# Decay tables of a recurrent-attention-plus-MLP kernel fetched as eight rows and spread by TensorE, and one rounding operation moved ahead of a read-out

## Chip, cores, metric

One core of one Trainium2 chip. The metric is device time in microseconds of one execution. All executions counted here are of the fast state (the one execution of the ladder has no state on record), and "the kernel before" is always the one run beside the others on the same chip. Three chips occur: one for the first comparison, one for the first four experiments, one for the other eight.

## The reference

A recurrent attention with a decay per head, whose output is the input of an MLP with leaky ReLU:

```python
gamma = 1.0 - 2.0 ** (-5.0 - np.arange(H, dtype=np.float32))
for t in range(S):                      # B, H, S, D = 4, 8, 768, 64
    state = gamma[None, :, None, None] * state + np.einsum('bhd,bhe->bhde', k[:, :, t], v[:, :, t])
    y[:, :, t] = scale * np.einsum('bhd,bhde->bhe', q[:, :, t], state)
# x = y as (3072, 512)
h = x @ w_in                            # 512 x 2048, given in float64
g = np.maximum(0.01 * h, h)
out = (g @ w_out).astype(np.float32)
```

## The kernel before

The sequence is worked in chunks of 128 tokens (C). The decays become three constant tables in one tile `dec` of 128 x 524 values: `gq` (512 columns, one per query position for each of four pairs of heads), `gk` (8 columns) and `gc` (4 columns). Start-up is a race: TensorE has nothing to multiply until queries and keys land, and the first projection step ("d", `direct`) needs both attention outputs and weights. The weights come as float64 words and are rounded to float32 by ScalarE (`powers`) and VectorE (`mantissas`), piece by piece. Fillers (`keep_busy`, on zeros) are there to bring TensorE's clock up.

```python
    load_qk(0, 0)
    nc.sync.dma_start(out=dec[:, rates:], in_=decay[:, rates:])     # gk, gc: 128 rows of 48 bytes
    load_v(0, 0)
    load_qk(0, 1)
    nc.sync.dma_start(out=dec[:, :rates], in_=decay[:, :rates])     # gq: 128 rows of 2 KB
    load_v(0, 1)
    load_piece(0)
    load_qk(0, 2)
    load_v(0, 2)
    load_piece(1)
    # ... cut
    keep_busy(7)
    score(0, 0)             # 16 matmuls on 64x64 quarters of the array
    masked(0, 0)            # VectorE, PSUM -> SBUF
    decay_v(0, 0, nc.vector)   # values times gk
    keep_busy(6)
    score(0, 1)
    values(0, 0)
    masked(0, 1)
    decay_v(0, 1, nc.vector)
    keep_busy(3)
    next_powers()           # ScalarE, weights piece 0
    taken(0, 0, x)          # the read-out: x = PSUM times gq
    values(0, 1)
    taken(0, 1, x)
    next_powers()
    next_mantissas()        # VectorE, three operations on piece 0
    score(0, 2)
    keep_busy(3)
    steps = direct(0, 0, x, parts[0][1], 0)
    next(steps)             # first d step
    next_mantissas()
    # ... cut: the second d step needs weights piece 1, and so on
```

## Time and profile before

| | before |
|---|---|
| median (3 runs) | 668.73 us (668.72 to 668.85) |
| time of the profiled execution | 669.81 us, span 667.9 us |
| TensorE busy | 660.5 us, 99% of the span |
| TensorE busy from 18.29 us to the end | 646.05 of 649.60 us |
| first d step, second d step | 16.00 us, 18.29 us |

Here is the start of TensorE's own timeline (start, length, engine, line, operation, what it writes and reads, array rows and columns used, shapes, count, idle time before):

```profile
1.40 3.17 PE L610 MATMUL idle<-t 128*128 128x512 bf16 x7 [1.40 <-DVE t L605]
4.49 1.99 PE L165 MATMUL ap<-qk 64*64 64x128 f32 x32
6.41 1.67 PE L610 MATMUL idle<-t 128*128 128x512 bf16 x6
```

Seven fillers took 3.17 us, the next six 1.67 us. The page's clock row prints full rate where it has no record yet.

### The profile page before, as it was taken

The page shows a single profiled execution, that of the slowest core. Times are in us where ns is not written, and L with a number is a line of the kernel's source. Part 1 is how long each engine was busy: PE and PEld are TensorE (multiplying, and loading weights), DVE is VectorE, ACT ScalarE, POOL GpSimd, SP SyncE. Part 2 cuts the span into 40 slices and gives each one's busy share as a digit, 9 for nine tenths or more (in the row PEclk, how much of TensorE's full clock was granted, in tenths as well). Part 3 has the DMA queues.
Part 4 walks back from the last instruction along what each step waited for, and adds up shares of the span by engine and source line. Part 5 has one row for each costly group of instructions (what it writes and reads, how often), then busy time and mean ns, then how long its engine had stood idle before and what let it go on. Part 6 is the DMA issues. An engine that isn't in the chain of part 4 may idle for free.

```text
span 667.9 us, 10403 instructions
## 1 busy us (share of the span) xinstructions
PE 660.5 (99%) x4507; PEld 573.1 (86%) x4507; DVE 371.9 (56%) x570; ACT 175.5 (26%) x321; POOL 19.6 (3%) x21
## 2 busy tenths in 40 slices
PE   7999999999999999999999999999999999999998
PEld 4888888888888888888888888888888888888886
DVE  4789869889889685314542613653531444341342
ACT  2864456255261002111201310210211220221210
POOL 0000000000000111000000100100100000000000
PEclk9999999999999999999999999999999999999999
DMA  8931322322421553003002200301300000000001
GB/s 320 405 113 32 121 69 64 98 92 65 157 64 65 189 190 127 1 0 104 25 16 82 93 1 1 127 1 64 127 1 0 2 0 33 31 1 1 0 1 63
DMA packets 16029, 49.17 MB, mean 74 GB/s; under 512 B 1904, under 2 KB 2160, under 8 KB 15984
## 3 DMA queue, kind: packets, MB, share of 16 engines
q1 hardware_dynamic: 15984, 48.51, 20.9%
q8 instruction: 35, 0.57, 0.3%
q14 instruction: 10, 0.08, 0.0%
HBM read 42.21 MB, written 6.29 MB: 73 GB/s over the span
## 4 chain that ended last, share of the span: by engine, by line
PE 97%; DMA 1%; SPq 1%; DVE 1%; ACT 0%; issue 0%; DVEq 0%
PE B_o L398 12%; PE A_o L398 12%; PE C_o L398 12%; PE C_h L398 12%; PE B_h L398 12%; PE A_h L398 12%; PE D_o L398 6%; PE D_h L398 6%; PE yp L193 3%; PE ap L165 3%; PE d L420 2%; PE yp L184 2%; DMA raw<-in_weights_dram 1%; PE yp L208 1%; PE sums L208 0%; SPq L134 0%
## 5 line engine op out<-in xcount | busy, mean ns | idle before, releaser
L398 PE MATMUL A_h<-x,w 128*128 128x256 f32 x368 | 86.9, 379 | 0.0
L398 PEld LDWEIGHTS A_h<-x,w 128*128 128x128 f32 x368 | 69.9, 190 | 9.5
L398 PE MATMUL A_o<-g,w 128*128 128x256 f32 x288 | 68.0, 379 | 0.0
L433 ACT ACTIVATE g<-g 128x512 f32<-128x512 f32 x69 | 42.0, 630 | 89.3 <-DVE g L347 89.3
L398 PEld LDWEIGHTS A_o<-g,w 128*128 128x128 f32 x288 | 54.7, 190 | 7.4
L438 ACT COPY m<-A_h 128x512 f32<-128x512 f32 x23 | 13.4, 583 | 141.2 <-PE A_h L398 101.6
L347 DVE TENSOR_TENSOR m<-m,B_h 128x512 f32<-128x512 f32 x23 | 15.7, 685 | 57.7 <-PE B_h L398 57.7
L347 DVE TENSOR_TENSOR m<-m,B_o 128x512 f32<-128x512 f32 x16 | 10.9, 684 | 63.9 <-PE B_o L398 63.9
L398 PE MATMUL C_h<-t,w 128*128 128x256 f32 x184 | 44.1, 382 | 0.0
L398 PE MATMUL B_h<-x,w 128*128 128x256 f32 x184 | 44.1, 382 | 0.0
L238 DVE TENSOR_TENSOR x<-yp,dec 128x512 f32<-128x512 f32 x24 | 16.4, 688 | 48.6 <-PE yp L208 34.2
L398 PE MATMUL B_h<-t,w 128*128 128x256 f32 x184 | 43.5, 379 | 0.0
L398 PE MATMUL C_h<-x,w 128*128 128x256 f32 x184 | 43.5, 379 | 0.0
L398 PE MATMUL D_h<-t,w 128*128 128x256 f32 x184 | 43.5, 379 | 0.0
L398 PEld LDWEIGHTS C_h<-t,w 128*128 128x128 f32 x184 | 34.5, 190 | 5.5 <-issue 0.9
L398 PEld LDWEIGHTS D_h<-t,w 128*128 128x128 f32 x184 | 35.0, 190 | 4.8
L398 PEld LDWEIGHTS C_h<-x,w 128*128 128x128 f32 x184 | 35.0, 190 | 4.8
L398 PEld LDWEIGHTS B_h<-t,w 128*128 128x128 f32 x184 | 35.0, 190 | 4.8
L398 PEld LDWEIGHTS B_h<-x,w 128*128 128x128 f32 x184 | 34.5, 190 | 5.1 <-issue 0.3
L350 DVE TENSOR_TENSOR gd<-g,gd 128x512 f32<-128x512 f32 x48 | 34.7, 722 | 1.6
L170 DVE TENSOR_TENSOR am<-ap,mask 128x1024 f32<-128x1024 f32 x24 | 28.5, 1219 | 12.0 <-PE ap L165 12.0
L398 PE MATMUL D_o<-gd,w 128*128 128x256 f32 x144 | 34.0, 379 | 0.0
(110 smaller groups left out, 1018.8 us busy)
## 6 DMA issues: line engine op xcount, KB each, us to landing
raw<-in_weights_dram SPq DMA_DIRECT2D x31, 512.0 KB, 4.0
qk<-in_qk_dram SPq DMA_DIRECT2D x19, 512.0 KB, 3.6
kv<-in_kv_dram SPq DMA_DIRECT2D x17, 512.0 KB, 4.6
out_dram<-o SPq DMA_DIRECT2D x23, 256.0 KB, 2.1
in<-in_qk_dram SPq DMA_DIRECT2D x3, 512.0 KB, 7.2
in<-in_kv_dram SPq DMA_DIRECT2D x3, 512.0 KB, 7.8
kv<-in_kv_dram SPq DMA_DIRECT2D x4, 256.0 KB, 7.5
o_in<-in_qk_dram SPq DMA_DIRECT2D x2, 512.0 KB, 9.0
```

The lines of the kernel that those rows point to most:

```text
L165: nc.tensor.matmul(ps[ts(u, 64), j, a, :], lhsT=x[ts(j, 64), 1, a, ts(u, 64)], rhs=x[ts(j, 64), 0, a, :])
L170: nc.vector.tensor_tensor(out=am.rearrange("p j a t -> p (j a) t"), in0=scores[c, b].rearrange("p j a t -> p (j a) t"), in1=mask.unsqueeze ...
L184: nc.tensor.matmul(ps[ts(i, 64), j, m, :], lhsT=st[b][ts(j, 64), a, :], rhs=x[ts(j, 64), 0, a, :], start=(m == 0), stop=False, skip_group_ ...
L193: nc.tensor.matmul(ps[ts(i, 64), j, m, :], lhsT=y[:, 1, 2 * a + j, :], rhs=am[:, j, a, :], start=(c == 0 and m == 0), stop=True, skip_grou ...
L208: nc.tensor.matmul(sp[ts(j, 64), a, :], lhsT=y[:, 0, 2 * a + j, :], rhs=y[:, 1, 2 * a + j, :], start=start, stop=True, skip_group_check=True)
L238: nc.vector.tensor_tensor(out=blocks, in0=ps[:, :, 0 : HP // 2, :], in1=gq, op=ALU.mult)
L347: nc.vector.tensor_tensor(out=out, in0=a, in1=b, op=ALU.add)
L350: nc.vector.tensor_tensor(out=out, in0=a, in1=b, op=ALU.subtract)
L398: nc.tensor.matmul(half, lhsT=block(w, sa)[:, k, ts(i, 128)], rhs=rhs[:, k, :], start=(first and (i == 0 or split) and n == 0 and k == 0), ...
L420: nc.tensor.matmul(banks[r][:, i, :], lhsT=block(2 * u, r + 2 * kh)[:, k, ts(i, 128)], rhs=x[:, 2 * kh + th, k, :], start=(step == 0 and i ...
L433: nc.scalar.activation(g[:, i], g[:, i], AF.Prelu, alpha=0.01)
L438: nc.scalar.copy(out=got["m1"], in_=ps)
```

## The change

The intent: take 262 KB of tables out of the transfers that stand ahead of the first weights. The host now gives eight rows (25 KB) that ScalarE's queue fetches into an unused part of `t`; TensorE multiplies them with rows of ones and zeros and so spreads them over 128 partitions; VectorE and ScalarE copy the results into `dec`. Four fillers go in exchange. Besides, the first of the three rounding operations of weights piece 0 is put ahead of the read-out that waits for TensorE.

```diff
-    load_qk(0, 0)
-    nc.sync.dma_start(out=dec[:, rates:], in_=decay[:, rates:])
-    load_v(0, 0)
-    load_qk(0, 1)
-    nc.sync.dma_start(out=dec[:, :rates], in_=decay[:, :rates])
-    load_v(0, 1)
+    nc.scalar.dma_start(out=rows, in_=decay)
+    load_qk(0, 0)
+    load_v(0, 0)
+    load_qk(0, 1)
+    load_v(0, 1)
 ... cut
-    keep_busy(7)
+    keep_busy(6)
+    nc.tensor.matmul(tables[:, 0, 0:H], lhsT=by_head, rhs=ones, ...)
+    nc.tensor.matmul(tables[:, 0, H : H + HP], lhsT=place, rhs=g_c, ...)
+    nc.vector.tensor_copy(out=dec[:, n_gq:], in_=tables[:, 0, 0 : H + HP])
     score(0, 0)
     masked(0, 0)
+    nc.tensor.matmul(spread, lhsT=place, rhs=g_q, ...)
+    nc.scalar.copy(out=dec[:, 0:n_gq], in_=spread)
     decay_v(0, 0, nc.vector)
-    keep_busy(6)
+    keep_busy(3)
     score(0, 1)
 ... cut
-    taken(0, 1, x)
+    next_mantissas(lambda: taken(0, 1, x))   # first operation, read-out, the other two
     next_powers()
-    next_mantissas()
```

## The prediction

> **What bounds the kernel now.** First the page of the kernel before: which engine is full, and when.
>
> ```profile
> PE 660.5 (99%) x4507; PEld 573.1 (86%) x4507; DVE 371.9 (56%) x570; ACT 175.5 (26%) x321; POOL 19.6 (3%) x21
> ...
> PE   7999999999999999999999999999999999999998
> ...
> DMA  8931322322421553003002200301300000000001
> ```
>
> TensorE is 99% busy; only the first slice (16.7 us) shows a 7, and only there and in the second are the DMA engines at 8 or 9 tenths. A change that touches start-up alone can win only what TensorE lacks there. To find where it starts to run without holes I read the chain of waits of the first 32 us (start, length, what):
>
> ```profile
> 5.72 9.18 DMA raw<-in_weights_dram
> 14.90 0.02 issue
> 14.93 0.67 ACT w L327
> 15.60 0.02 issue
> 15.62 0.64 ACT z L329
> 16.26 0.02 issue
> 16.28 0.44 DVE w L339
> ...
> 16.74 0.70 DVE w L341
> ...
> 17.54 0.70 DVE w L343
> 18.25 0.04 issue
> 18.29 1.99 PE d L420 x8
> 20.28 1.02 PE yp L193 x16
> ```
>
> The reader sees that the end is set by one transfer, the second weight piece. It lands at 14.90, is rounded (ScalarE, then VectorE, 3.35 us), and releases the second step of the first projection, "d", at 18.29. From there on the chain is TensorE after TensorE, with one 1.3 us VectorE piece near 42 us that follows TensorE's own scores. The table of busy time by stretch agrees: from 18.29 to 667.89 TensorE is busy 646.05 of 649.60 us. So **whatever moves that second d step moves the end by as much, until another wait takes over.**
>
> The timeline of VectorE shows what holds the first d step (16.00), the next candidate:
>
> ```profile
> 12.04 0.69 DVE L238 TENSOR_TENSOR x<-yp,dec 128x512 f32<-128x512 f32 x1
> 13.40 0.69 DVE L238 TENSOR_TENSOR x<-yp,dec 128x512 f32<-128x512 f32 x1 [0.68 <-PE yp L193]
> 14.01 0.42 DVE L339 TENSOR_SCALAR w<-raw 128x512 uint32<-128x512 uint32 x1
> 14.46 0.69 DVE L341 SCALAR_TENSOR_TENSOR w<-raw,w 128x512 f32<-128x512 uint32 x1
> 15.26 0.69 DVE L343 SCALAR_TENSOR_TENSOR w<-w,z 128x512 f32<-128x512 f32 x1
> ```
>
> VectorE idles 0.68 us before the second read-out (L238), with the first rounding (L339, L341, L343) queued behind it. Last, the first DMA issues:
>
> ```profile
> 1.24 0.42 SPq L574 DMA_DIRECT2D dec<-decay_dram  x1
> ...
> 2.65 0.43 SPq L577 DMA_DIRECT2D dec<-decay_dram  x1
> ...
> 3.60 0.43 SPq L288 DMA_DIRECT2D raw<-in_weights_dram  x1
> ```
>
> Both tables of decays stand ahead of the first weights. By the times from issue to landing of the single transfers (issue plus landing time): first queries and keys 4.3, small table 4.5, first values 6.1, second queries and keys 9.1, big table 9.75, second values 10.4, first weights 11.7, second weights 14.9.
>
> **What the Trainium skill says.** "DMA: Bandwidth & Descriptors", "Issuing engines are not separate DMA queues": transfers from different issuing engines run on the same 16 DMA engines, and a second issuer saves only sequencer time. The trace before has one queue, so it can't confirm this; it makes me count the bytes removed, not the second queue, as the gain. The same page, "Queues, rings and completion order": on each DMA engine descriptors are taken in ring order. The trace agrees: landings come in the order of issue, and from 8 us on 512 KB take about 1.3 us (11.7, 13.0 for the next two such transfers). The same page, "Why small descriptors are slow (HBM only)" makes the 128 rows of 48 bytes of the small table suspect; but that table landed 0.17 us after the transfer ahead of it, so I count it as little. "TensorE: Matmul & The Clock Gate", "What's actually happening": the array runs at half rate until it has been busy for about 3.4 us, and falls back after an idle window. The trace agrees for the ramp: the first 32 score matmuls took 1.99 us (from 4.49), the next 32 1.10 us (from 9.13). That is what the filler matmuls are for, so I check that the change opens no long hole.
>
> **The change part by part.**
>
> 1. *Table transfers leave the main queue.* Removed: 6 KB in 48-byte rows and 256 KB in 2 KB rows. In the stretch from 8 to 12 us the DMA engines move 418 GB/s with share 1.04, so 262 KB are worth 0.63 us there; the small table lies in a stretch (4 to 8 us) at share 0.84, and I give it 0.1. Added: eight rows of 780 values, 25 KB, 0.06 us at that rate. Net 0.67 us for everything behind the big table in the queue, which includes both first weight pieces. The stretch from 4 to 8 us moved only 290 GB/s; I [...]allow 0.1 us more: **about 0.75 us earlier**, first weights about 10.95, second about 14.15. The second queries and keys have only the small table ahead of them, so I leave them at 9.1 (perhaps 0.2 earlier).
>
> 2. *SyncE issues two transfers fewer* (0.47 us each with their gaps); ScalarE issues one instead, before its table load of 1.28 us, in a time when it is idle until 11.7. The queue is filled well ahead of the data, so this is worth nothing by itself. The waits to reuse a DMA semaphore also shift: the second weights wait for the rows instead of the small table, the third for the first queries and keys; all those land earlier than needed.
>
> 3. *Spreading.* TensorE gets three single-precision matmuls (128x8, 128x4, 128x512) and loses 4 of 19 fillers (7+6+3+3 become 6+3+3+3). A single-precision 128x256 matmul follows the next after 1.73/8 = 0.216 us, so 512 columns are about 0.43 us; three fillers are 3 x 0.278 = 0.83 us (from 1.67 us for six). By my estimate the rows land near 3 us (first packets about 1 us after issue, as for the first transfer[...]), while six fillers end near 4.1, so the scores still start about 4.5. Scores end about 6.5, spread and fillers about 7.8, then TensorE waits for the second queries and keys until 9.1: a hole of 1.3 us where there was one of 1.06. Short of 3.4 us, so the clock should hold. VectorE gets a copy of 12 columns (idle until 6.62), ScalarE a copy of 128x512, 0.58 us as the 128x512 copies of the page, done before 8.5, while the first read-out that needs it is at 12.04. **All of it off the path, 0 us.**
>
> 4. *First rounding's first operation ahead of the second read-out.* It goes into the 0.68 us hole: it can start when VectorE is free at 12.73 and when ScalarE's second pass (which reads what it overwrites) is done. That pass ended 13.05; with weights 0.75 earlier it ends 12.3. So L339 runs 12.7 to 13.1, the read-out stays at 13.40, L341 starts 14.01 instead of 14.46, L343 ends 15.5 instead of 15.95: **first d step at 15.55 instead of 16.00**. Without part 1, L339 would run 13.1 to 13.5 and push the read-out by 0.1.
>
> *Sum.* The second d step needs the later of two: first d step plus its own length, 15.55 + 1.94 = 17.5; and its weights, 18.29 - 0.75 = 17.54. They meet, so the gain is 0.75 us, and part 4 is what lets part 1 through: with the transfers alone the first d step stays near 16.0, the second at 17.95, and the gain is about 0.35. With part 4 alone the second d step still waits for its data: about 0. After it, third weights and the scaling by ScalarE hang on the same chain and the same queue, and move along. Slack there is small (the third d step had its weights at 22.03 and started at 22.27), but it is relative slack, so it stays.
>
> **The rivals.** *A. The gain is held by the front:* the second queries and keys land later (the rows share engines with them) or the hole lets the clock fall, so that scores and values run at half rate (up to 1 us each). Against: 25 KB are 0.06 us, and a hole of 1.06 us did no harm. That would give 668.3 to 669.3. *B. More than the bytes:* the slow stretch from 4 to 8 us was due to the tables, the second queries and keys come 0.5 us or more earlier, and with them the first d step. For it: 290 GB/s against 418. Against: the small table cost 0.17 us. That would give 667.3. *C. Hidden anyway:* later loads or ScalarE's scaling set the third or fourth d step and swallow the gain, giving 668.5. Against: from 18.29 on TensorE has no hole that ends on a transfer. *D. The rows land late* (5 us or more), holding TensorE's queue in front of the scores; harmless up to about 6 us, since the second scores wait until 9.1 anyway.
>
> **Range and chances.** 668.73 - 0.75 = **667.98 us**. Low end: B, 667.4; high end: gain mostly held by a new wait, 668.6; three runs before spread 0.13 us. Two per cent would be 13.4 us, more than all the idle time TensorE has (7.4 us), and no part can cost that: faster by over 2% 0.005, within 2% 0.99, slower by over 2% 0.005.
>
> **What would show it.** Part 1: second weights land near 14.15, first near 10.95. Part 3: rows landed before 4.1, all matmuls after 6.5 at full rate, ScalarE's copy done before 8.5. Part 4: L339 before the second L238, first d step near 15.55. Sum: second d step near 17.55 and no hole of TensorE after it but the one near 42 us; TensorE's busy time from there unchanged near 646 us. Wrong, if the weights land earlier by the bytes and the second d step does not follow, if a new hole opens after it, or if the second queries and keys move by more than 0.3 us.

## The result

The changed kernel took 670.80 us in the median of six runs, the kernel before 668.73 us (now six runs, 668.50 to 669.44); the ratio is 1.0023 (95% interval 1.0004 to 1.0042). That is "same" at 2%, but outside the predicted range, and on the other side. The six runs are not one cluster: five lie at 670.65 to 671.41 us, one at 667.64 us. From here on, "slow" and "fast" executions mean these two clusters.

The changed kernel's page, the lines that answer to the first ones of the prediction:

```profile
PE 663.4 (99%) x4509; PEld 574.8 (86%) x4509; DVE 374.6 (56%) x571; ACT 175.9 (26%) x322; POOL 19.5 (3%) x21
...
PE   9999999999999999999999999999999999999998
```

TensorE's first slice went from 7 to 9. It looks like a better filled engine; it is an engine that takes longer for the same work, as the chain of waits of the first 18 us tells (start, length, what):

```profile
4.13 0.52 PE tables L635 x2
4.65 0.42 PE tables L637 x2
5.07 1.92 PE ap L165 x32
6.99 2.00 PE spread L642 x2
8.99 1.39 PE idle L624 x3
10.38 1.87 PE ap L165 x32
...
16.77 0.70 DVE w L357
...
17.52 3.85 PE d L434 x16
```

There is no transfer left in this chain. The reader is to see three things. The spread took 2.00 us. Three fillers took 1.39 us (six had taken 1.67 before), and the second scores 1.87 us where they took 1.10: the clock was at half rate until about 12 us. And the two d steps run as one (x16, from 17.52): the second follows the first at once, at about 19.4 us, so it no longer waits for its weights but for TensorE. The trace's first record of full rate begins at 11.97 us, against 6.84 before.

The moved operation did what it was moved for (VectorE's timeline):

```profile
14.62 0.42 DVE L346 TENSOR_SCALAR w<-raw 128x512 uint32<-128x512 uint32 x1
15.38 0.69 DVE L238 TENSOR_TENSOR x<-yp,dec 128x512 f32<-128x512 f32 x1 [0.34 <-PE yp L193]
```

And the transfers came much earlier than predicted: second queries and keys 7.55 us (before 9.09), first weights 9.49 (11.70), second weights 12.75 (14.90).

### The profile page after: what moved, and what is told of

Read it like the earlier page. It is cut to its first block, busy times and chain, and to the rows that moved or that the text cites. A ratio compares the mean times of both kernels' runs of the same rounds, so it can differ in the third digit from the quotient of the medians.

```text
span 669.0 us, 10408 instructions
## 1 busy us (share of the span) xinstructions
PE 663.4 (99%) x4509; PEld 574.8 (86%) x4509; DVE 374.6 (56%) x571; ACT 175.9 (26%) x322; POOL 19.5 (3%) x21
## 4 chain that ended last, share of the span: by engine, by line
PE 99%; DVE 1%; issue 0%; DVEq 0%
PE B_o L412 12%; PE A_o L412 12%; PE C_o L412 12%; PE C_h L412 12%; PE B_h L412 12%; PE A_h L412 12%; PE D_o L412 6%; PE D_h L412 6%; PE ap L165 3%; PE yp L193 3%; PE d L434 2%; PE yp L184 2%; PE yp L208 1%; PE idle L624 1%; DVE am L170 0%; PE sums L208 0%
```

## Experiments

**Theory.** The transfers and the order gain, but the matmuls of eight rows keep the clock at half rate, so TensorE's front becomes the bound. **Rivals.** The new order on VectorE costs the time; the fillers that were taken away cost it; the earlier transfers are luck of one trace.

### The transfers and the order without TensorE's part (rows_alone)

```diff
-    (three matmuls and both copies)
+    nc.vector.memset(dec, 0.125)
-    keep_busy(6) ... keep_busy(3)
+    keep_busy(7) ... keep_busy(6)
```

> The transfers of the change and the moved rounding operation, without TensorE's work: the three spreading matmuls and both copies are left out, the fillers are 7 and 6 again, the tables are filled with a constant by VectorE (wrong result on purpose). Theory (the transfers gain about 2 us, and the front of TensorE's queue loses more than that): second queries and keys near 7.6, second weights near 12.8, clock granted near 7 us, second d step near 16.1 to 16.5, so 666.5 to 667.0 us. Rival (the transfers never gain more than the predicted 0.75 us; the earlier landings are luck of one trace): second weights near 14.1, 668.0 us.

Measured: 667.78 us (667.67 to 668.09), kernel before 669.35 (this chip's spread is wider: 668.17 to 670.15), ratio 0.9979 (0.9967 to 0.9991); the result is wrong on purpose. TensorE's timeline:

```profile
7.46 1.10 PE L165 MATMUL ap<-qk 64*64 64x128 f32 x32 [0.29 <-DMA qk<-in_qk_dram]
...
13.88 1.99 PE L434 MATMUL d<-x,w 128*128 128x256 f32 x8 [0.39 <-DVE w L357]
16.36 1.99 PE L434 MATMUL d<-x,w 128*128 128x256 f32 x8 [0.49 <-DVE w L357]
```

The second scores start when their data land and run at full rate, and the second d step starts at 16.36. So the transfers and the order together gain 1.4 us (0.21% of 669), and what the change lost on top of that is TensorE's part with its two copies. The absolute times expected were 1 us too low, because they were counted from the trace before, which was a late one.

### TensorE's part without the transfers (dummy8, dummy128)

The kernel before with the same matmuls as dummies on zeros; the two kernels differ in the number of rows alone.

```diff
-    keep_busy(7); score(0, 0); masked(0, 0); decay_v(0, 0); keep_busy(6)
+    keep_busy(6); single(8); single(4); score(0, 0); masked(0, 0)
+    single(256); single(256); decay_v(0, 0); keep_busy(3)
+    # single(n): lhsT = zeros[0:k, 0:128], rhs = zeros[0:k, 0:n], k = 8 or 128
```

> The kernel before with TensorE's front of the changed kernel put in as dummies on zeros: after 6 fillers two tiny single-precision matmuls of 8 rows, after the first scores two 8-row matmuls of 256 columns, then 3 fillers; transfers as before. Theory (these matmuls keep the clock at half rate): three fillers after the dummies take 1.3 us, second scores take 1.9 us and end near 12.2, second d step near 20, so about 670.5 us. Rival (TensorE's front is harmless, the loss comes from the transfers or VectorE's order): 668.7 us.

> As the 8-row dummies, but all of 128 rows: same count, columns and type. If the clock grant weighs how many rows of the array work, the clock is granted near 7 us, the dummies of 512 columns take about 0.9 us, and the time is 668.7 to 669.2 us. If it is the time in which the small matmuls wait on each other, or the order alone, it is as slow as with 8 rows, about 670.5 us.

Measured: with 8 rows 670.61 us in the median, in two clusters (669.08, 669.19, 669.81 and 671.42, 671.72, 671.91), ratio 1.0019 (1.0003 to 1.0035). With 128 rows 669.74 us, 668.59 to 670.61, ratio 1.0008 (0.9995 to 1.0022); none above 671. Both profiles happened to fall on executions that got the clock early (full rate from 4.12 and 4.36 us), so their traces tell nothing of the slow cluster. The times say that TensorE's part alone makes slow executions; half of the 8-row executions escape. They only point to the rows: the two intervals overlap, and three of the five 128-row executions lie at 669.7 to 670.6 us, so 8 and 128 rows are not told apart here.

### The clock's rule by itself (ladder)

```diff
+    for k in (8, 32, 64, 96, 128):
+        20 matmuls of k rows, 512 bf16 columns, on zeros
+    24 single-precision matmuls of 128 rows by 8 columns, on zeros
     keep_busy(7)
```

> One look at the clock's rule; the kernel before with dummies on zeros ahead of its fillers: 20 matmuls of 512 bfloat16 columns each with 8, 32, 64, 96 and 128 rows in turn (cold 0.427 us apart, so 8.5 us each, at full rate 0.216 us), then 24 single-precision matmuls of 128 rows by 8 columns, then the 7 fillers. If the grant weighs the rows that work, the 8-row block stays 0.427 us apart for its whole 8.5 us and the spacing halves only in a block of more rows. If it counts time in which matmuls run, the spacing halves within the 8-row block[...]. If small matmuls that wait on each other let the clock fall, the fillers behind them are 0.427 us apart again.

The table of busy time by stretch (stretch, length, TensorE busy and its number of records, weight loads, and so on; the third number from the end is the clock, which again prints 1.00 where there is no record yet). The first three stretches lie in the blocks of 8, 32 and 64 rows, the fourth and fifth in those of 96 and 128, the sixth in the small matmuls, the seventh in the fillers behind them:

```profile
2.00:9.00 7.00, 7.00 (x17) 2.34 (x16) 0.00 (x0) 0.08 (x1) 0.00 (x0) 1.00 0.91 306
10.50:17.50 7.00, 7.00 (x18) 2.34 (x16) 0.00 (x0) 5.25 (x13) 0.00 (x0) 1.00 1.03 408
19.00:26.00 7.00, 7.00 (x18) 2.48 (x17) 0.00 (x0) 1.39 (x3) 0.00 (x0) 1.00 0.88 345
28.00:33.00 5.00, 5.00 (x13) 1.82 (x12) 0.00 (x0) 0.00 (x0) 0.00 (x0) 1.00 0.01 3
34.00:38.00 4.00, 4.00 (x20) 1.76 (x19) 0.00 (x0) 0.00 (x0) 0.00 (x0) 1.00 0.00 0
40.00:43.00 3.00, 3.00 (x29) 3.00 (x28) 0.00 (x0) 0.00 (x0) 0.00 (x0) 1.00 0.00 0
45.00:47.00 2.00, 2.00 (x6) 0.76 (x5) 0.00 (x0) 0.00 (x0) 0.00 (x0) 0.50 0.00 0
```

TensorE is busy all the time, yet 17 or 18 records fit into 7 us with 8, 32 and 64 rows (0.427 us apart, half rate), and 20 into 4 us (0.216 us apart) after the clock came, which was at 33.35 us, 6.1 us into the 96 rows. Under the small matmuls it went again, at 43.59, though they had all 128 rows and left no hole: six fillers in 2 us are half rate again. It came back at 50.42. Those changes are 10.24 and 6.83 us apart: three and two times 3.41 us.

This fits one rule: in free-running windows of 3.41 us, the share of the array's rows times the time in which they stream must reach a threshold. The windows are well supported: in the ladder and in the twelve other traces that have clock records, the time from the last grant to the fall at the end is a whole multiple (192 to 195) of 3.413 us.

The shares are counted from the starts of the records. In the ladder, the window that granted was all 96 rows, 75%; the one before it held 0.5 us of 64 rows and 2.7 us of 96 rows, 67%, and did not; nor did the one from 43.59 to 47.01 us, with small matmuls and then 2.35 us of full fillers, 69%. Before: the window from 3.43 to 6.84 us was full but for 0.14 us and granted; the one ahead of it was 60% and did not. Changed: from 1.73 to 5.14 us the fillers give 2.2 us and the first scores 0.14 us (68%), and the small tables hardly count; from 5.14 to 8.56 the scores give 1.8 us (52%), and eight rows of the spread hardly count; from 8.56 to 11.97 fillers and scores are 86%, and the clock came.

At the edge it is less clear. The dummies of 8 rows got it at 4.12 us with 2.54 us of fillers, 74%. But the order undone (below) did not get it at 3.95 us, where by its later grant at 14.19 us a window ended with the same 2.54 us of fillers. That window ended 0.02 us after the last filler, the granting one 0.19 us after; whether the counting lags the records by so much is not shown. So 69% never granted, and 74% once did and once did not: the threshold lies near there. That it is rows times time is an inference from these cases; zeros as data are common to fillers and ladder.

### How often, and on another chip (after_again)

> The changed kernel unedited, beside the other runs of one chip, for the share of slow executions. The ladder showed windows of 3.41 us that grant the clock only if about three quarters of the rows' time in one is worked. Before the small tables there are 2.5 us of full fillers (74% of a window), so only windows that end between about 3.9 and 4.8 us can grant: one execution in four. Those should take about 667.6 to 668.5 us, the others 670.5 to 671.5 us, 1.5 to 2 us over the kernel before in the mean. Rival (the slow ones belong to one chip): all near 668 us here.

Measured: five executions at 670.85 to 671.21 us, one at 667.66; kernel before 669.33; ratio 1.0015 (0.9997 to 1.0033). With the first comparison, 10 of 12 executions are slow and 2 are fast, at 667.64 and 667.66: less than the one in four expected from the windows, and too few to call it different. The two clusters are a property of this kernel and not of a chip.

### The small tables behind the first scores (tables_later)

```diff
     keep_busy(6)
-    tables, tables, copy
     score(0, 0)
     masked(0, 0)
+    tables, tables, copy
     spread, copy
```

> The changed kernel with the two small table matmuls and their copy moved behind the first scores, so that fillers and first scores run without a break as before. If the break of 0.94 us at 4.1 us costs the clock its first window: clock granted near 7 us, spread of about 0.9 to 1.5 us, second scores from about 8.5 to 9.6, 667 to 668 us, with few slow runs. If the spread of 8 rows alone is enough to hold the clock: second scores still take 1.9 us, 670.5 us or more.

Measured: 668.43 us (667.70 to 668.47), kernel before 669.35, ratio 0.9985 (0.9973 to 0.9997), no slow execution among five. TensorE's timeline:

```profile
6.05 0.38 PE L637 MATMUL tables<-t 8*128 8x8 f32 x2
6.29 0.36 PE L639 MATMUL tables<-t 8*128 8x4 f32 x2
6.51 1.10 PE L642 MATMUL spread<-t 8*128 8x512 f32 x2
```

The same three matmuls, moved by one block, take 1.5 us in place of 2.9 us, since fillers and scores now make 4.0 us of full work ahead of them, with one hole of 0.7 us (full rate from 5.51 us). Changing nothing but this position turns the loss of 0.2% into a gain of 0.15%. This is the test that carries the theory. (The trace of this run got the clock before it reached the tables. Five executions can't say that none is ever slow: by my estimate from the intervals above, with the scores at their cold length of 1.92 us, windows that start between 3.3 and 3.9 us, about a fifth of them, would still miss.)

### The fillers back (fillers_back)

```diff
-    keep_busy(6) ... keep_busy(3)
+    keep_busy(7) ... keep_busy(6)
```

> The changed kernel with 7 and 6 fillers as before in place of 6 and 3. If it was the missing fillers that lost the clock, all executions are near 668 us. If the matmuls of few rows lose it, slow executions stay: the seventh filler widens the first stretch to 3.0 us, so 4 in 10 get the clock early, and those that don't pay four more cold fillers, 1.7 us: up to 672.5 us.

Measured: 672.10 us (671.82 to 672.29), ratio 1.0041 (1.0027 to 1.0054), no fast one among four. The rival falls: with all fillers back the change is slower still, since cold fillers are only more work in front of the scores. Four in ten had been expected to escape; none of four did.

### The order undone, and the order alone (no_order, order_only)

```diff
 no_order: the changed kernel with
-    next_mantissas(lambda: taken(0, 1, x)); next_powers()
+    taken(0, 1, x); next_powers(); next_mantissas()
 order_only: the kernel before with the opposite edit
```

> The changed kernel with the first rounding's first operation back behind the second read-out. In a slow execution the first d step hangs on VectorE behind the second scores, so the 0.42 us of that operation come back: about 0.4 us over the changed kernel in slow executions (671.0 to 671.6 us), 0 to 0.4 us in fast ones. Rival (the new order makes VectorE wait for ScalarE and is part of the loss): 0.3 us or more under the changed kernel.

> The kernel before with the first rounding's first operation ahead of the second read-out and nothing else. The first d step starts 0.4 to 0.5 us earlier relative to the second queries' landing, the second still waits for the second weights: 0.0 to 0.2 us under the kernel before. Rival (the order is what costs the time): 1 us or more over it.

Measured, order undone: three slow executions (671.35 to 671.88 us) and three fast (667.85 to 668.20). Three fast ones of six, against two of twelve of the changed kernel, are too few to say that the order bears on the clock. Each cluster lies above that of the changed kernel on this chip, by 0.6 us (mean 671.63 against 671.00) and by 0.2 to 0.5 us (against the one at 667.66). The median, 669.77, would have said the opposite: it depends on how many executions got the clock. Its profiled execution shows how late the clock can come; here it was granted at 14.19 us, and the first values were cold too, so part of the 0.6 us may be the clock and not the order (TensorE's timeline):

```profile
10.31 1.99 PE L165 MATMUL ap<-qk 64*64 64x128 f32 x32
12.22 1.97 PE L193 MATMUL yp<-am,kv 128*64 128x128 f32 x16
```

The order alone: 668.82 us against 669.38, ratio 0.9992 (0.9980 to 1.0005): a gain of perhaps 0.5 us, not told from none.

### Each table's transfer alone (no_small, no_big)

Both are the order alone with one of the two table transfers left out and a constant in its place.

```diff
 no_small:
-    nc.sync.dma_start(out=dec[:, rates:], in_=decay[:, rates:])
+    nc.vector.memset(dec[:, rates:], 0.125)
 no_big:
-    nc.sync.dma_start(out=dec[:, :rates], in_=decay[:, :rates])
+    nc.vector.memset(dec[:, :rates], 0.125)
```

> As the order alone, without the transfer of the small table (128 rows of 48 bytes); its place is filled with a constant by VectorE (wrong result on purpose). By its bytes this is worth nothing; if 48-byte rows hold up the start of the transfers behind them, second queries and keys and second weights land 0.5 us or more earlier and the time falls by 0.4 to 0.8 us against the order alone.

> As the order alone, without the transfer of the big table (256 KB); constant in its place (wrong result on purpose). By its bytes (0.63 us at 418 GB/s) the weights land 0.65 us earlier and the time falls by about 0.6 us against the order alone; together with the small table this has to make up the 1.4 us or so by which the landings of the changed kernel beat those of before.

Measured: without the small table 668.66 us, ratio 0.9985 (0.9971 to 0.9999); without the big one 668.26 us, ratio 0.9979 (0.9967 to 0.9992); the order alone was 0.9992. So the big table is worth about 0.13%, 0.9 us, and the small one perhaps 0.5 us, with overlapping intervals. ScalarE's first pass over the second weights shows when these had landed, first with both tables in the queue (the order alone), then without the big one (ScalarE's timelines):

```profile
13.34 0.67 ACT L334 ACTIVATE w<-raw 128x512 f32<-128x512 uint16 x1 [1.25 <-DMA raw<-in_weights_dram]
```

```profile
12.43 0.67 ACT L334 ACTIVATE w<-raw 128x512 f32<-128x512 uint16 x1 [1.24 <-DMA raw<-in_weights_dram]
```

That is 0.91 us. But with the same two tables in the queue the second weights landed at 14.90 in the trace before and at 13.3 here, and without the small table they landed at 13.85, later than with it. Single landings vary by as much as the tables are worth; why stays open. All kept traces together answer the rival that the earlier transfers are luck of one trace: ScalarE's first pass over the second weights starts at 13.34 to 14.93 us in the four with both tables in the queue (mean 14.31), and at 12.75 to 13.28 us in the six with the rows in their place and the same order of loads (mean 13.02). That is 1.3 us of the 2.15 us by which the first two traces differ; the rest is a late trace before.

### A better version (best)

```diff
     load_qk(0, 2)
+    load_piece(1)
     load_v(0, 2)
-    load_piece(1)
 ... cut
-    keep_busy(6); tables, tables, copy; score(0, 0); masked(0, 0)
-    spread, copy; decay_v(0, 0); keep_busy(3); score(0, 1)
+    keep_busy(7); score(0, 0); masked(0, 0); tables, tables, copy
+    decay_v(0, 0); keep_busy(4); score(0, 1); spread, copy
     values(0, 0); masked(0, 1); decay_v(0, 1)
-    keep_busy(3)
```

> An attempt at a better version: the changed kernel with 7 fillers straight into the first scores, then the small tables and 4 fillers, the big spread behind the second scores where TensorE has to wait for VectorE anyway, the 3 fillers there dropped, and the second weights ahead of the third values in SyncE's queue. The clock should be granted by 7 us in nearly every execution; first d step near 14 us, second near 15.9 us: 667.0 to 667.6 us where the kernel before takes 669.3, under the 667.8 us of the transfers alone. If the second weights do not bound it any more, it stays at about 667.8 us; if the clock is missed, single executions lie above 669 us.

Measured: 667.58 us (667.24 to 667.99, six runs), kernel before 669.33, ratio 0.9975 (0.9962 to 0.9987), correct, no slow execution. It beats the kernel before, and the changed one by 3.4 us in the median. Most of that is the clock: the changed kernel's two fast executions (667.64 and 667.66 us) are as short. Nor is it told from the transfers and the order alone (0.9979, overlapping intervals). TensorE's timeline:

```profile
7.46 1.10 PE L165 MATMUL ap<-qk 64*64 64x128 f32 x32
8.49 1.12 PE L645 MATMUL spread<-t 8*128 8x512 f32 x2
9.55 2.15 PE L193 MATMUL yp<-am,kv 128*64 128x128 f32 x32
...
13.99 3.86 PE L434 MATMUL d<-x,w 128*128 128x256 f32 x16 [0.51 <-DVE w L357]
```

The spread stands where the three fillers stood, the second values follow the first without a wait, and the second weights no longer bound the second d step (x16 in one piece).

## Why the prediction was wrong

**What bounds the kernel, and where a gain comes from:** held. In every trace but the ladder's, from the second d step to the end takes 649.6 to 649.7 us. Changed: 17.52 plus half of 3.85 is 19.4 us, 1.1 us after 18.29, and the span grew by 1.1 us.

**Part 1, "about 0.75 us earlier":** the size was about right for the part as timed: the transfers alone beat the order alone by about 0.13% (0.9979 against 0.9992, from two chips, overlapping intervals), 0.9 us; by the landings of all traces it is 1.3 us. The small table was worth perhaps 0.5 us where 0.1 was given to it. What the prediction missed is that its trace of before was 1.1 us over the median run, with late landings, so that the two traces show 2.15 us.

**Part 3, "All of it off the path, 0 us":** this is the step that failed, in three terms.
- *"so the clock should hold"*: it was taken for granted that the clock comes at all. The Trainium skill's rule of about 3.4 us ("TensorE: Matmul & The Clock Gate", "What's actually happening") was read as time in which matmuls run. In the ladder 8, 32 and 64 rows did not bring it, and small matmuls lost it. The clock came at 11.97 us in place of 6.84, and after 14 us in an execution of the kernel with the order undone; the front was worked at half rate.
- *"so 512 columns are about 0.43 us"*: the spread took 2.00 us at half rate and 1.06 to 1.1 us at full rate. The 1.73 us of a step had been divided by eight records, but a step is four matmuls with two records each (as its "32 score matmuls" are 16). The Trainium skill, "FP8 and Floating Point Precision", "TensorE Precision Notes", would have told: true single precision takes four passes through the array. By an estimate from that page and the 0.216 us that 512 bfloat16 columns of the fillers take at full rate, four passes are 0.86 us; 1.73/4 for 256 columns gives the same.
- *"the scores still start about 4.5"*: the small tables took 0.94 us on TensorE ahead of the scores, which started at 5.0. The rows had landed in time: the 8-row dummies, which need none, started at 4.07 us too, the tables at 4.06. The matmuls themselves had no line in the sum.

Together the second scores started at 10.31, not at the 9.1 of the prediction, when their data had been there since 7.55.

**Part 4, "first d step at 15.55 instead of 16.00":** the mechanism held. The operation runs in the hole ahead of the second read-out, and undoing it costs 0.2 to 0.6 us by a few executions of each cluster. "With part 4 alone ... about 0" was measured as 0.9992, 0.5 us or nothing.

**The rivals.** Rival A had named this cause ("the hole lets the clock fall") and was dismissed because a hole of 1.06 us had done no harm. The hole was not the danger: with no hole at all the clock did not come. B was partly right: the second queries and keys landed at 7.55 us, but single landings vary (7.47 to 9.09 us in the four traces with both tables, 7.08 to 7.71 in the six with the rows). C did not happen. D did not happen: full fillers ran to 3.93 us and the tables followed at once.

**The range** allowed 0.1 us below the kernel before; the slow executions lie 2.1 us above it, the fast ones (667.64) 0.3 us under the predicted time, of which no trace was kept. A kernel whose executions form two clusters has no time that one number could hit.

## What to carry to other kernels

By the rule inferred here, a filler matmul is worth its rows times its columns: before exchanging fillers for small matmuls ahead of the moment when the clock comes, add up the array's working share in every 3.4 us, and place such matmuls behind that moment, where they also cost half (1.5 us against 2.9 here). When an engine's busy share rises and the time doesn't fall, compare the length of equal instructions before looking for new work. Look at all runs and not at the median where they form clusters, and check whether the execution that was profiled is a typical one.

## What the Trainium skill lacked or had wrong

- "TensorE: Matmul & The Clock Gate", "What's actually happening", speaks of how busy the array is and of time; it lacks that the working rows count. Blocks of 8, 32 and 64 rows, each 8.5 us without a hole, stayed at half rate (0.427 us per 512 columns); the clock came 6.1 us into 96 rows. Windows of up to 69% did not grant; of two with 74%, one did and one did not.
- The same section has the busy state follow from "≥1 busy SHORT window (~3.4µs sustained)". Here the clock was granted once with 2.54 us of full work in a window (at 4.12 us), though not every time, and taken away after small matmuls that left no hole (8 columns, 128 rows, 0.11 us apart). Its windows of 3413 ns, free-running, are confirmed: changes 10.24 and 6.83 us apart, and whole multiples from grant to fall in every trace with clock records.
- The same page warns that the run-to-run phase shifts the ramp and calls the penalty under 1%. It stayed under 1% here, but made two clusters 3.2 us apart (667.64 and 670.8 us), more than the change was worth.
